# A third group's first layer by seven products, with sums made sooner and keys decayed on another engine

## Chip, cores, metric

One NeuronCore of a Trainium2 chip. The metric is device time in microseconds for one launch. Three runs of the kernel before gave 205.46, 205.52 and 206.92; their median is 205.52.

## What is computed

A linear attention with decay, then a two-layer network with the Mish activation. The attention has batch 4, 8 heads, 768 positions and 64 dimensions; the reference goes through the positions in blocks with a running state for each head:

```python
intra = np.einsum('bhic,bhjc->bhij', qb, kb) * Dmask[None]
intra = np.einsum('bhij,bhjd->bhid', intra, vb)
inter = np.einsum('bhid,bhde->bhie', qb * lam_pow[None], kv_state)
out[:, :, sl] = intra + inter
kb_dec = kb * rev_pow[None]
kv_state = lam_block[None, :, None, None] * kv_state + np.einsum('bhsd,bhse->bhde', kb_dec, vb)
...
x = attn_out.transpose(0, 2, 1, 3).reshape(B * S, H * D)     # 3072 x 512
h = x @ w_in                                                 # 512 -> 2048
g = h * np.tanh(sp)                                          # sp = log(1 + exp(h))
return (g @ w_out).astype(np.float32)                        # 2048 -> 512
```

## The kernel before

The order of the work is written out by hand: each engine runs its instructions in the order of the Python text, and waits only for data and for buffers.

**Groups.** The 768 positions are six groups of 128 (n = 0 to 5). A group has four batches, so 512 tokens. For each group there is attention (for each batch b), a first layer (512 -> 2048, sixteen slices of 128 outputs, Mish on ScalarE) and a second layer (2048 -> 512). "First group" is n = 0, "third group" n = 2.

**Attention of one batch.** `scores` (L250): 8 small matmuls into two PSUM banks, then VectorE multiplies each bank by the mask into `sb` (L260). `outputs` (L272): matmuls of the queries with the state, and of `sb` with the values, into one bank; VectorE scales them into `xn` (L284). `xn` is turned into the columns of `xt`, by a DMA on SP's queue (L287) or by TensorE in a function called later (L290 to L295). `state` (L299): matmuls of the decayed keys `kd` with the values (L302); VectorE adds the old state into `raw` (L310, two buffers); a multiplication by `lbm` writes the new state (L312). That last step is on GpSimd, but for batches 0 and 1 of the second group it is on VectorE and is called later (`decays1`). `decay_k` (L246) makes `kd` from the keys, with four buffers, on the engine that it is given. Keys and queries are turned by TensorE (`turn_pe`, L221) or, two batches at a time, by DMAs on SP's queue (`turn_dma`, L239). Keys, queries and values are fetched two batches at a time by DMAs on GpSimd's queue (`load_pair`, L84).

**First layer, two ways.** A plain `unit` (L337) is one slice of 128 outputs: 4 matmuls of 128 x 128 by 512 columns into one bank (L329), then Mish (L335). `two_units` (L348) does two slices for half the tokens. The other way (`set_of` to `set_step`, L392 to L448) takes four slices at a time as a 2 x 2 block product with seven products in place of eight, each of 4 matmuls by 256 columns (L412). A set needs sums of tokens (`x_sums`, L379, four VectorE operations for a group) and sums of weights (`w_sum`, L367, four for each quarter of w_in, made once). Its steps are m1; seed, a copy by ScalarE of the bank into a second bank (L426); m2; m5 with a copy by ScalarE (L434); m6 with a VectorE addition (L437); m7 with another (L441); m3; m4. Four sets make a group.

**Second layer.** The first group's is plain (L574). From the second on it has seven products, cut into fourteen halves of 8 matmuls (`dense2`, L529); one call of `h()` issues one half. It needs sums of w_out (`weight_sum`, L458, VectorE, eight in all) and of the tokens (`token_sum`, L471, called by `sums`).

**The loop** (L814, n = 1 to 4) weaves in each turn the second layer of group n, the first layer of group n + 1 and the attention of group n + 2. KINDS says for each turn and set whether the first layer is plain ("p") or by seven products ("s"): turn 1, which is the third group's first layer, is "pppp", the others "ssss". In an "s" turn the calls `opening`, `mm`, `closing` and `settle` set the steps of the sets among the halves; `held` keeps a `state` back to the next `s_`. Turn 1 also makes the sums of w_in for quarters 1 and 3 (WSUMS) and the last two `weight_sum`. Ahead of the loop, L715 to L801 write out the attention of the second and third groups, the second group's first layer by `two_units`, and the first group's second layer.

Of the kernel before, what the change touches and what calls it, by code (L numbers as in the profile page):

```python
# [7 lines left out]
F32 = mybir.dt.float32  # L8
# [12 lines left out]
def kernel(  # L21
# [276 lines left out]

    def state(n, b, tag, eng, later=False):  # L299
        pv = bank(tag, [JP, 128])  # L300
# [5 lines left out]
        if n == 0:  # L306
            nc.vector.tensor_tensor(out=w_new, in0=pv, in1=lbm, op=ALU.mult)
        else:
            raw = work.tile([128, JP, 128], F32, name="raw", tag="raw", bufs=2)
            nc.vector.tensor_tensor(out=raw, in0=pv, in1=wst[n, b], op=ALU.add)  # L310
            wst[n + 1, b] = w_new
            decay = lambda: eng.tensor_tensor(out=w_new, in0=raw, in1=lbm, op=ALU.mult)  # L312
            return decay if later else decay()
# [371 lines left out]
    def out1(b, turn, po, pv):  # L685
        later[b] = outputs(1, b, turn, po)
        return state(1, b, pv, nc.vector if b < 2 else nc.gpsimd, b < 2)

# [26 lines left out]
    turn1(2, "ze")  # L715
    turn1(3, "oB")
    two_units(1, 0, 0)
    scores(1, 2)
    for decay in decays1:
        decay()  # L720
    decay_k(1, 2, nc.vector)
    two_units(1, 2, 0)
    two_units(1, 4, 0)
    scores(1, 3)
    out1(2, "G", "z", "H")
    decay_k(1, 3, nc.vector)
    two_units(1, 6, 0)
    later[2]()
    out1(3, "G", "e", "o")
    two_units(1, 8, 0)  # L730
    later[3]()
    two_units(1, 10, 0)
    turn_pe(2, 0, ("H", "z"))
    decay_k(2, 0, nc.vector)
    decay_k(2, 1, nc.vector)
    w_sum(0, 0, nc.vector)
    w_sum(0, 1, nc.vector)
    two_units(1, 12, 0)
# [11 lines left out]
    two_units(1, 0, 1)  # L750
    w_sum(0, 2, nc.vector)
    w_sum(0, 3, nc.vector)
    turn_pe(2, 1, ("H", "G"))
# [19 lines left out]
    w_sum(2, 3, nc.vector)  # L773

# [23 lines left out]
    plain2(3, 0, 1, 2, 3)  # L798
    sums(1, 0, 2, 3)
    busy(1)  # L800
    halves = dense2(1)  # L801
# [8 lines left out]

    KINDS = {1: "pppp", 2: "ssss", 3: "ssss", 4: "ssss"}
    WSUMS = {(1, 0): (1,), (1, 1): (3,)}

    for n in range(1, NG - 1):  # L814
# [37 lines left out]
        def ws(n, i):  # L852
            for x in WSUMS.get((n, i), ()):
                for t in range(4):
                    w_sum(x, t, nc.vector)

# [67 lines left out]


        if "s" in kinds:
            x_sums(n + 1, 0, 1, 2, 3)
        opening(0)
        if m < NG:
            turn_dma(m, 1)  # L930
        if kinds[0] == "s":
            h(1)
            mm(0, "m2", "m5", "m6")
            sums(n, 1, 0, 1)
            h(1)
            o_(0)
            fetch(("k", 0), ("q", 0))
            closing(0)
        else:
            u(0)  # L940
            sums(n, 1, 0, 1)
            if n == 1:
                weight_sum(3, 0)
                weight_sum(3, 1)
            h(1)
            u(1)
            h(1)
            u(2)
            o_(0)
            fetch(("k", 0), ("q", 0))  # L950
            u(3)


        opening(1)
        h(1)
        if kinds[1] == "s":
            settle()
            mm(1, "m2")
            h(1)
            mm(1, "m5", "m6")  # L960
            sums(n, 1, 2)
            h(1)
            o_(1)
            fetch(("v", 0), ("k", 1))
            closing(1)
        else:
            u(8)
            settle()
            s_(1)
            sums(n, 1, 2, 3)  # L970
            ws(n, 0)
            h(1)
            u(9, 10)
            o_(1)
            fetch(("v", 0), ("k", 1))
            h(1)
            u(11)

# [7 lines left out]
        if kinds[2] == "s":  # L986
# [7 lines left out]
            h(1)  # L994
        else:
            u(4)
            settle()
            s_(2)
            u(5)
            ws(n, 1)  # L1000
            h(1)
            u(6)
            o_(2)
            fetch(("q", 1), ("v", 1))
            h(1)
            sums(n + 1, 0, 0, 1)
            h(1)
            u(7)


        opening(3)
        if kinds[3] == "s":
# [9 lines left out]
            sums(n + 1, 0, 2, 3)  # L1022
        else:
            s_(3)
            h(1)
            u(12)
            settle()
            h(1)
            o_(3)
            u(13)  # L1030
            sums(n + 1, 0, 2, 3)
            h(1)
            u(14)
        more = n + 1 < NG - 1
# [3 lines left out]
        if kinds[3] == "s":  # L1038
            if more:
                h(1)  # L1040
            settle()
        else:
            settle()
            u(15)
            if more:
                h(1)

# [32 lines left out]
```

## Time and profile before

| | |
|---|---|
| median of three runs | 205.52 us |
| the profiled execution | 206.36 us, of which 204.6 is the span of the profile |
| TensorE (PE) busy in the span | 193.8 us |
| VectorE (DVE) busy | 147.5 us |
| ScalarE (ACT) busy | 98.5 us |
| GpSimd (POOL) busy | 81.7 us |
| granted TensorE clock | 0.999 |

The profile's busy time of PE counts matmuls from issue to a modelled end, so neighbouring matmuls overlap; what one costs in a stream is the distance from its start to the next one's. PEld is the loading of weights, which overlaps PE. A row of a timeline gives start, length, engine, line, operation, output and inputs, how often, and in brackets how long the engine was idle before it and what ended that. "x2" is two operations one after the other in one row. GpSimd's DMA rows are the time that it takes to issue a transfer, not the transfer.

### The profile page before, as it was taken

What the parts mean: (1) busy time and instruction counts of PE and PEld (TensorE: products, weight loads), DVE (VectorE), ACT (ScalarE), POOL (GpSimd) and SP (SyncE); (2) the same over time, 40 slices, a digit from 0 to 9 for tenths busy, and PEclk for the clock granted to TensorE, in tenths of its full rate; (3) what the DMA queues carried; (4) which work ended last, traced back from release to release, by engine and by line L of the source; (5) the groups of instructions that cost most, each with busy time, mean ns of one, the idle gap of its engine ahead of it and who ended that gap; (6) DMA issues with size and microseconds to landing.
All of it is one profiled execution on the core that took longest, in us unless ns stands there. A gap on an engine that the chain in (4) does not pass through costs nothing.

```text
span 204.6 us, 4668 instructions
## 1 busy us (share of the span) xinstructions
PE 193.8 (95%) x1931; PEld 149.1 (73%) x1931; DVE 147.5 (72%) x247; ACT 98.5 (48%) x176; POOL 81.7 (40%) x78
## 2 busy tenths in 40 slices
PE   7869998979999999999999999999999999999990
PEld 3657455768865556667668888988988988888890
DVE  6696557698896977589868698799588657179041
ACT  4775663728631125343245662465474484826300
POOL 7998452472272591648684368230000000000020
PEclk9999999999999999999999999999999999999999
DMA  8999999999999999699999999994113211003123
GB/s 129 137 142 204 175 177 156 162 207 194 142 141 131 223 167 176 159 108 115 161 212 194 137 77 130 172 211 112 29 26 80 77 54 53 0 3 113 47 100 104
DMA packets 109336, 26.26 MB, mean 128 GB/s; under 512 B 99458, under 2 KB 108802, under 8 KB 109314
## 3 DMA queue, kind: packets, MB, share of 16 engines
q0 software_dynamic: 77568, 13.37, 88.5%
q1 hardware_dynamic: 30704, 12.33, 29.0%
q10 hardware_dynamic: 1042, 0.26, 0.6%
q8 instruction: 15, 0.25, 0.5%
q14 instruction: 7, 0.06, 0.1%
HBM read 27.26 MB, written 6.29 MB: 164 GB/s over the span
## 4 chain that ended last, share of the span: by engine, by line
PE 76%; DMA 9%; POOL 7%; DVE 3%; ACT 2%; issue 1%; POOLq 0%; DVEq 0%; ACTq 0%
PE bG L523 15%; PE bH L523 13%; DMA vn<-in_v_dram 8%; PE bB L412 6%; PE bC L412 5%; PE bA L412 4%; PE bA L329 3%; PE bB L329 3%; PE be L255 2%; PE bC L355 2%; POOL win L96 2%; PE bC L329 2%; PE bz L281 2%; PE bA L574 2%; PE bA L355 2%; PE bB L355 2%
## 5 line engine op out<-in xcount | busy, mean ns | idle before, releaser
L312 POOL TENSOR_TENSOR w<-raw,lbm 128x512 f16<-128x512 f32 x14 | 20.4, 1458 | 43.0 <-DVE raw L310 42.8
L523 PEld LDWEIGHTS <-gsum 128*128 128x128 f16 x336 | 31.2, 98 | 4.3
L523 PEld LDWEIGHTS <-hsg 128*128 128x128 f16 x240 | 23.0, 98 | 4.4
L605 POOL TENSOR_TENSOR c<-p,u 128x512 f32<-128x512 f32 x1 | 1.3, 1272 | 58.7 <-DVE p L604 58.7
L260 DVE TENSOR_TENSOR sb<-be,dm 128x512 f16<-128x512 f32 x22 | 15.1, 686 | 8.8 <-PE bo L255 8.1
L523 PE MATMUL bH<-tsum,gsum 128*128 128x256 f16 x160 | 20.4, 273 | 0.0
L329 PEld LDWEIGHTS <-win 128*128 128x128 f16 x136 | 12.6, 98 | 10.3 <-DMA win<-in_moe_w_in_dram 0.5
L412 PEld LDWEIGHTS <-wsum 128*128 128x128 f16 x192 | 18.5, 98 | 2.1
L523 PE MATMUL bG<-wout,hsg 128*128 128x256 f16 x160 | 19.9, 273 | 0.0
L412 PEld LDWEIGHTS <-win 128*128 128x128 f16 x144 | 13.8, 98 | 2.2 <-issue 0.5
L486 DVE TENSOR_TENSOR gsum<-hsg 128x1024 f16<-128x1024 f16 x20 | 15.1, 759 | 0.0
L284 DVE TENSOR_TENSOR xn<-bz,lq 128x512 f16<-128x512 f32 x18 | 12.3, 686 | 3.7 <-PE bz L281 3.7
L260 DVE TENSOR_TENSOR sb<-bo,dm 128x512 f16<-128x512 f32 x22 | 15.0, 680 | 0.0
L355 PEld LDWEIGHTS <-win 128*128 128x128 f16 x128 | 12.0, 98 | 1.6
L87 POOL DMA_DIRECT2D kn<-in_k_dram x10 | 11.8, 1182 | 2.8 <-PE bB L329 1.5
L87 POOL DMA_DIRECT2D qn<-in_q_dram x10 | 11.7, 1170 | 1.7 <-PE bA L329 0.9
L87 POOL DMA_DIRECT2D vn<-in_v_dram x10 | 11.6, 1164 | 1.4 <-DMA win<-in_moe_w_in_dram 1.4
L412 PE MATMUL bA<-xt,win 128*128 128x256 f16 x80 | 12.0, 272 | 0.1
L416 ACT ACTIVATE hsg<-bC 128x512 f16<-128x512 f32 x10 | 5.9, 593 | 11.7 <-PE bC L412 11.7
L329 PE MATMUL bA<-xt,win 128*128 128x512 f16 x44 | 11.3, 380 | 0.0
L574 PEld LDWEIGHTS <-hsg 128*128 128x128 f16 x64 | 6.1, 98 | 6.8
L335 ACT ACTIVATE hsg<-bA 128x512 f16<-128x512 f32 x11 | 6.6, 597 | 9.2 <-PE bA L329 9.2
(189 smaller groups left out, 442.3 us busy)
## 6 DMA issues: line engine op xcount, KB each, us to landing
out_dram<-osum SPq DMA_DIRECT2D x23, 256.0 KB, 2.8
kn<-in_k_dram POOLq DMA_DIRECT2D x10, 256.0 KB, 9.0
qn<-in_q_dram POOLq DMA_DIRECT2D x10, 256.0 KB, 7.1
vn<-in_v_dram POOLq DMA_DIRECT2D x10, 256.0 KB, 8.6
wout<-in_moe_w_out_dram POOLq DMA_DIRECT2D x4, 512.0 KB, 15.4
win<-in_moe_w_in_dram POOLq DMA_DIRECT2D x3, 512.0 KB, 10.8
vz<-in_v_dram POOLq DMA_DIRECT2D x2, 256.0 KB, 6.8
kn<-in_k_dram POOLq DMA_DIRECT2D x3, 128.0 KB, 4.7
```

What stands on the lines that cost most here:

```text
L87: nc.gpsimd.dma_start(out=tile_, in_=rows(src, n, 2 * bp, 2))
L260: nc.vector.tensor_tensor(out=sb[n, b, t], in0=p_[t], in1=dm[:, t], op=ALU.mult)
L284: nc.vector.tensor_tensor(out=xn, in0=po, in1=bc(lq, 2, D), op=ALU.mult)
L312: decay = lambda: eng.tensor_tensor(out=w_new, in0=raw, in1=lbm, op=ALU.mult)
L329: nc.tensor.matmul(open_[n, ni][:, lo:hi], win[ni // 4][:, kc, (ni % 4) * 128 : (ni % 4) * 128 + 128], xt[n][:, kc, lo:hi], start=(opens a ...
L335: nc.scalar.activation(h_tile(n)[:, ni, :], open_.pop((n, ni)), AF.Mish)
L355: nc.tensor.matmul(t[:, u, :], win[ni // 4][:, kc, m : m + 128], xt[n][:, kc, cs], start=(u == 0 and kc == 0), stop=(kc == NKC - 1), skip_ ...
L412: nc.tensor.matmul(t[:, u, :], lhs, rhs, start=(fresh and u == 0 and kk == 0), stop=(kk == 1), skip_group_check=True)
L416: nc.scalar.activation(h_tile(o.n)[:, 4 * o.s + 2 * r : 4 * o.s + 2 * r + 2, t * HC : t * HC + HC], src, AF.Mish)
L486: nc.vector.tensor_tensor(out=gsum[n, i][:, ks, :], in0=a, in1=b, op=op)
L523: nc.tensor.matmul(t, lhs(kk, blk), rhs(kk)[:, lo:hi], start=(fresh and kk == 0), stop=(kk == HK - 1), skip_group_check=True)
L574: nc.tensor.matmul(po, hsg[n][:, ki, b * C : (b + 1) * C], wout[part][:, kk, :], start=(ki == 0), stop=(ki == NKI - 1))
```

## The change

Turn 1 of the loop, the third group's first layer, uses seven products as well. All sums of w_in are therefore made ahead of the loop, in an order of quarters 0, 2, 1, 3 in which the sets need them. The third group's keys are decayed by GpSimd instead of VectorE, at other places in its queue. The second group's state decays for batches 0 and 1 stay on VectorE, but behind the masks of all four batches, and kd(1,2) goes ahead of scores(1,2). The sums `raw` of batches 2 and 3 of the second group use the buffers `p5` and `c22`. The first turn has an order of its own (`fresh`): it makes token sums of the second layer first, opens the first set, then makes the four token sums `x_sums`, and sets a half between m2 and m5. The branches of plain units are removed from the loop; they did nothing in the other turns.

```diff
-    def state(n, b, tag, eng, later=False):
+    def state(n, b, tag, eng, later=False, home=("raw", 2)):
...
-            raw = work.tile([128, JP, 128], F32, name="raw", tag="raw", bufs=2)
+            raw = work.tile([128, JP, 128], F32, name="raw", tag=home[0], bufs=home[1])
...
-        return state(1, b, pv, nc.vector if b < 2 else nc.gpsimd, b < 2)
+        return state(1, b, pv, nc.vector if b < 2 else nc.gpsimd, b < 2,
+                     ("raw", 2) if b < 2 else (("p5", "c22")[b - 2], 1))
...
     turn1(3, "oB")
+    decay_k(1, 2, nc.vector)
     two_units(1, 0, 0)
     scores(1, 2)
-    for decay in decays1:
-        decay()
-    decay_k(1, 2, nc.vector)
     two_units(1, 2, 0)
     two_units(1, 4, 0)
     scores(1, 3)
+    decay_k(2, 0, nc.gpsimd)
     out1(2, "G", "z", "H")
     decay_k(1, 3, nc.vector)
     two_units(1, 6, 0)
     later[2]()
     out1(3, "G", "e", "o")
+    for decay in decays1:
+        decay()
     two_units(1, 8, 0)
     later[3]()
     two_units(1, 10, 0)
     turn_pe(2, 0, ("H", "z"))
-    decay_k(2, 0, nc.vector)
-    decay_k(2, 1, nc.vector)
-    w_sum(0, 0, nc.vector)
-    w_sum(0, 1, nc.vector)
+    decay_k(2, 1, nc.gpsimd)
+    for i in range(4):
+        w_sum(0, i, nc.vector)
...
     two_units(1, 0, 1)
-    w_sum(0, 2, nc.vector)
-    w_sum(0, 3, nc.vector)
+    w_sum(1, 0, nc.vector)
+    w_sum(1, 1, nc.vector)
...
     attended(2, 1)
+    decay_k(2, 2, nc.gpsimd)
     for t, bp in (("k", 0), ("q", 0), ("v", 0)):
         load_pair(t, 3, bp)
+    decay_k(2, 3, nc.gpsimd)
...
-    w_sum(2, 0, nc.vector)
-    w_sum(2, 1, nc.vector)
-    w_sum(2, 2, nc.vector)
-    w_sum(2, 3, nc.vector)
+    for i in range(4):
+        w_sum(2, i, nc.vector)
+    w_sum(1, 2, nc.vector)
+    w_sum(1, 3, nc.vector)
...
     attend(2, 2)
-    decay_k(2, 2, nc.vector)
+    w_sum(3, 0, nc.vector)
+    w_sum(3, 1, nc.vector)
     plain2(1, 0, 1)
     attended(2, 2)
     turn_dma(3, 0)
     attend(2, 3)
-    decay_k(2, 3, nc.vector)
+    w_sum(3, 2, nc.vector)
+    w_sum(3, 3, nc.vector)
...
     sums(1, 0, 2, 3)
+    weight_sum(3, 0)
     busy(1)
     halves = dense2(1)
...
-    KINDS = {1: "pppp", 2: "ssss", 3: "ssss", 4: "ssss"}
-    WSUMS = {(1, 0): (1,), (1, 1): (3,)}
+    KINDS = {0: "pppp", 1: "ssss", 2: "ssss", 3: "ssss", 4: "ssss"}
...
+        fresh = kinds[0] == "s" and KINDS[n - 1][3] == "p"
+        if fresh:
+            sums(n, 1, 0, 1)
+            opening(0)
         if "s" in kinds:
             x_sums(n + 1, 0, 1, 2, 3)
-        opening(0)
+        if not fresh:
+            opening(0)
         if m < NG:
             turn_dma(m, 1)
         if kinds[0] == "s":
             h(1)
-            mm(0, "m2", "m5", "m6")
-            sums(n, 1, 0, 1)
-            h(1)
+            if fresh:
+                mm(0, "m2")
+                h(1)
+                mm(0, "m5", "m6")
+            else:
+                mm(0, "m2", "m5", "m6")
+                sums(n, 1, 0, 1)
+                h(1)
             o_(0)
             fetch(("k", 0), ("q", 0))
+            if fresh:
+                h(1)
             closing(0)
...
         opening(1)
-        h(1)
+        if not fresh:
+            h(1)
         if kinds[1] == "s":
             settle()
+            if n == 1:
+                weight_sum(3, 1)
             mm(1, "m2")
```

More of the change, by code (lines that the diff above doesn't have):

```diff
@@ L850, in fetch @@
                     load_pair(t, m + 1, bp)
[L852 to L855, printed above, removed]
         kinds = KINDS[n]
@@ L932 @@
             h(1)
-            mm(0, "m2", "m5", "m6")
-            sums(n, 1, 0, 1)
-            h(1)
+            if fresh:
[6 more added lines that the diff above has]
+                h(1)
             o_(0)
             fetch(("k", 0), ("q", 0))
+            if fresh:
+                h(1)
             closing(0)
[L939 to L944, printed above, removed]
-            h(1)
-            u(1)
-            h(1)
[L948 to L955, printed above, removed]
+        opening(1)
+        if not fresh:
+            h(1)
         if kinds[1] == "s":
             settle()
+            if n == 1:
+                weight_sum(3, 1)
             mm(1, "m2")
@@ L965 @@
             closing(1)
[L966 to L977, printed above, removed]
         opening(2)
@@ L994 @@
             h(1)
[L995 to L1008, printed above, removed]
         opening(3)
@@ L1022 @@
             sums(n + 1, 0, 2, 3)
[L1023 to L1033, printed above, removed]
         more = n + 1 < NG - 1
@@ L1041 @@
             settle()
[L1042 to L1046, printed above, removed]
     sums(NG - 1, 1, 2, 0, 1, 3)
```

## The prediction, made before the changed kernel ran

> **What bounds the kernel now.** I read the page's busy table and chain, then the windows by stage, then the timelines of TensorE, VectorE and GpSimd between 38 and 80 us.
>
> ```profile
> PE 193.8 (95%) x1931; PEld 149.1 (73%) x1931; DVE 147.5 (72%) x247; ACT 98.5 (48%) x176; POOL 81.7 (40%) x78
> PE 76%; DMA 9%; POOL 7%; DVE 3%; ACT 2%; issue 1%; POOLq 0%; DVEq 0%; ACTq 0%
> ```
> ```profile
> 32.80:58.80 26.00, 24.69 (x309) 20.48 (x306) 22.25 (x36) 15.04 (x27) 11.65 (x10) 1.00 1.87 171
> 58.80:75.07 16.27, 16.27 (x116) 8.16 (x114) 14.20 (x21) 2.52 (x5) 10.01 (x9) 1.00 1.43 171
> 75.07:107.20 32.13, 32.13 (x289) 21.98 (x288) 24.21 (x39) 12.39 (x21) 19.92 (x17) 1.00 1.69 153
> 107.20:135.90 28.70, 28.70 (x320) 25.03 (x318) 23.28 (x39) 14.54 (x26) 14.20 (x13) 1.00 1.47 149
> ```
>
> The columns of the windows are length, then busy time of PE, PEld, DVE, ACT, POOL, granted clock, DMA. TensorE sets the end: it is busy in all of 58.8 to 135.9 at a granted clock of 1.00, so a matmul saved there is time saved, if nothing makes it wait instead. The loop's turn that the change rewrites is 75.07 to 107.20; the next turn, 107.20 to 135.90, already does with the fourth group what the change does with the third. The other place is 32.8 to 58.8, where TensorE is 1.31 us short of full. Its three waits are all for VectorE:
>
> ```profile
> 41.58 0.40 PE L302 MATMUL bH<-vn,kd 128*128 128x128 f16 x4 [0.44 <-DVE kd L248]
> 43.38 0.40 PE L293 MATMUL bG<-ident,xn 128*128 128x128 f16 x4 [0.53 <-DVE xn L284]
> 44.58 0.40 PE L302 MATMUL bo<-vn,kd 128*128 128x128 f16 x4 [0.34 <-DVE kd L248]
> ```
>
> **The matmuls.** Four matmuls of 512 columns make a unit (L329); four of 256 make one step of the seven products (L412).
>
> ```profile
> 78.99 0.86 PE bB L329 x4
> 109.08 0.44 PE bA L412 x4
> ```
>
> 16 units at 0.866 (from the start-to-start of these rows' neighbours) are 13.86 us; 4 sets of 7 steps at 0.436 are 12.21. The change removes **1.65 us** of TensorE work. Four steps cost two 512-column matmuls' time each, so nothing is lost to the narrower shape. The Trainium skill, "TensorE: Matmul & The Clock Gate", section "Back-to-back issue gap", gives 131 ns as the sustained spacing of 512-column matmuls; by that the 64 old matmuls would be 8.4 us and the change a loss. The rows have 215 ns, so the rule does not hold here and enters below only as a rival.
>
> One wait comes with it. In the same place of a later turn, the second step of the first set waits for the copy that seeds the other bank: 136.99 plus 0.87 of work is 137.87, and m2 starts at 138.09.
>
> ```profile
> 136.99 1.05 PE L523 MATMUL bG<-wout,hsg 128*128 128x256 f16 x8
> 138.09 0.60 PE L412 MATMUL bA<-xt,win 128*128 128x256 f16 x4
> ```
>
> The old turn ended with a unit, so the turn after it had no old set to close and no such wait; now it has: **+0.2**.
>
> **The evictions.** Each set adds two VectorE additions, two ScalarE copies; the group adds four token sums.
>
> ```profile
> L437 DVE TENSOR_TENSOR bC<-bB,p 128x512 f32<-128x512 f32 x6 | 4.2, 700 | 5.9 <-PE bB L412 5.4 <-ACT p L434 0.5
> L390 DVE TENSOR_TENSOR xsum<-xt,xsum 128x512 f16<-128x512 f16 x6 | 2.5, 421 | 0.1
> L375 DVE TENSOR_TENSOR wsum<-win 128x512 f16<-128x512 f16 x8 | 4.2, 522 | 0.0
> ```
>
> VectorE gets 8 x 0.69 + 4 x 0.42 = 7.2 us, and loses eight sums of w_in (some 4.2 at the last row's mean) and a tsum and two gsum, which move ahead (1.9). That makes 24.21 + 7.2 - 6.1 = 25.3 of some 30.5 us, the share of the following turn (23.28 of 28.70), in which TensorE does not wait. ScalarE gets two copies a set and comes to about the following turn's share, 14.54 of 28.70. Hidden, at 0, once the turn is under way.
>
> **What moves ahead of the turn.** Here the two engines collide. A VectorE operation on SBUF alone stands still while GpSimd computes; one that reads PSUM does not.
>
> ```profile
> 57.20 2.36 DVE L467 TENSOR_TENSOR tsum<-wout,tsum 128x1024 f16<-128x1024 f16 x2
> 57.37 1.65 POOL L312 TENSOR_TENSOR w<-raw,lbm 128x512 f16<-128x512 f32 x1 [2.46 <-DVE raw L310]
> 44.44 0.68 DVE L284 TENSOR_TENSOR xn<-be,lq 128x512 f16<-128x512 f32 x1
> 44.01 1.64 POOL L312 TENSOR_TENSOR w<-raw,lbm 128x512 f16<-128x512 f32 x1 [1.21 <-DVE raw L310]
> ```
>
> Two tsum should take 1.2 (0.60 from start to start); they take 2.36, and GpSimd 1.65 instead of 1.27: each waits for the other's whole operation, in turn. So keys moved to GpSimd (1.03 us alone) are not simply gone from VectorE: each can hold up one of its SBUF operations by up to 1.03, against the 0.60 to 0.68 that VectorE saves.
>
> ```profile
> L248 POOL TENSOR_TENSOR kd<-kn,lk x8: 1032/1130/1601, 75.1 to 123.8; 128x512 f16<-128x512 f16 x8
> 41.65 1.15 POOL L87 DMA_DIRECT2D vn<-in_v_dram  x1
> ```
>
> The second group, 38 to 46. Before, VectorE ran the two state decays and kd(1,2) ahead of the masks of scores(1,3):
>
> ```profile
> 38.44 0.69 DVE L260 TENSOR_TENSOR sb<-be,dm 128x512 f16<-128x512 f32 x1 [0.90 <-PE bo L255]
> 39.64 1.28 DVE L312 TENSOR_TENSOR w<-raw,lbm 128x512 f16<-128x512 f32 x2
> 40.84 0.68 DVE L248 TENSOR_TENSOR kd<-kn,lk 128x512 f16<-128x512 f16 x1
> 43.84 0.68 DVE L248 TENSOR_TENSOR kd<-kn,lk 128x512 f16<-128x512 f16 x1
> 45.64 2.36 DVE L248 TENSOR_TENSOR kd<-kn,lk 128x512 f16<-128x512 f16 x2
> 40.37 0.22 PE L255 MATMUL bo<-qT,kT 64*128 64x128 f16 x1
> ```
>
> After, kd(1,2) fits into VectorE's 0.90 of idle time before 38.44, and the 0.44 wait goes. The last score matmul ends at 40.59, so the masks start at 40.62; at 0.60 from start to start xn follows at 41.82, raw at 42.42, and kd(1,3) would at 43.02, ending 43.70: the state matmuls at 43.76 instead of 44.58, **-0.82**. But GpSimd now has kd(2,0) in its queue where it used to wait for raw. It is free at 42.80, 0.2 us ahead of kd(1,3), so kd(1,3) stands until 43.83 and ends at 44.51. The matmuls then start at 44.57: **0.0**. Ends of this term: -1.31 (all waits go) and +0.5 (kd(1,3) behind two GpSimd operations). I take 0.0, since 42.80 comes ahead of 43.02 in these rows. Behind kd(2,0) in GpSimd's queue stands the decay of state (1,2), some 0.4 us later for it; the state is read next at 64, so nobody waits. That the sums raw of (1,2) and (1,3) lie in two other buffers costs nothing: the first set takes these after 79.
>
> From 45 to 62: VectorE loses two keys (2.36 with the wait) and gets two decays and two sums. The decays read SBUF twice in f32. No row shows such an operation beside GpSimd, so its hold-up is between 0 and one GpSimd operation (1.27). With it, VectorE reaches the masks of scores(2,0) at 50.55, about 1 us later, and has them at 51.83, where TensorE comes for them. Nothing to 0.1. The Trainium skill's "SBUF — State Buffer", section "Who interferes with whom", counts any VectorE operation with two SBUF inputs, f32 too; by it the 1.27 applies, and the sum stays the same. Later six sums replace four ahead of scores(2,2); kd(2,2) on GpSimd, after the decay at 57.37, costs one hold-up: VectorE arrives at 62.9 where it used to wait 1.59 us until 62.62.
>
> ```profile
> 51.83 0.40 PE L281 MATMUL bz<-vn,sb 128*128 128x64 f16 x8
> 62.62 0.69 DVE L260 TENSOR_TENSOR sb<-be,dm 128x512 f16<-128x512 f32 x1 [1.59 <-PE bo L255]
> 63.83 0.68 DVE L248 TENSOR_TENSOR kd<-kn,lk 128x512 f16<-128x512 f16 x1
> 68.19 0.40 PE L281 MATMUL bz<-vn,sb 128*128 128x64 f16 x8
> ```
>
> From 62 to 69: Sums of w_in stand where kd(2,2) and kd(2,3) stood, 0.75 for 0.60, and kd(2,3) on GpSimd falls on the first pair, +1.0. The masks of scores(2,3) end at 68.35 where TensorE wants them at 68.19: **+0.2**. On GpSimd's queue the three loads of the fourth group go 1.6 us later (one key and its wait for the port). Issued at 60.6, landing 9 us on, transposed 4.5 to 4.9 us on, the last is there by about 76 for scores(3,0) at 77.1; on SP's queue the transposes only follow. Hidden with some 1 us to spare; without it, what is short is paid.
>
> ```profile
> kn<-in_k_dram POOLq DMA_DIRECT2D x10, 256.0 KB, 9.0
> kT<-kn SPq DMA_TRANSPOSE x7, 4.5
> ```
>
> From 69 to 80: VectorE runs 1.1 us late from here, through this:
>
> ```profile
> 70.54 1.64 DVE L486 TENSOR_TENSOR gsum<-gsum,hsg 128x1024 f16<-128x1024 f16 x1
> 72.11 1.52 DVE L467 TENSOR_TENSOR tsum<-wout,wout 128x1024 f16<-128x1024 f16 x1
> 73.56 1.52 DVE L486 TENSOR_TENSOR gsum<-hsg 128x1024 f16<-128x1024 f16 x1
> 75.00 0.68 DVE L486 TENSOR_TENSOR gsum<-hsg,gsum 128x1024 f16<-128x1024 f16 x1
> 75.08 2.50 POOL L248 TENSOR_TENSOR kd<-kn,lk 128x512 f16<-128x512 f16 x2
> 77.18 0.69 DVE L260 TENSOR_TENSOR sb<-be,dm 128x512 f16<-128x512 f32 x1 [1.49 <-PE bo L255]
> ```
>
> The slack ahead of the masks was 1.49. The change puts one tsum and two gsum there (1.8), and the two GpSimd keys then fall among them. The two rows of 1.52 are explained by no GpSimd computation (it was issuing loads, which slow no other row of their kind). If they become 0.60 at their new offsets, the masks run at 78.0 and the first token sums are there at 79.7 and 80.05; TensorE comes to m5 at 79.85 and to m6 at 80.3: **0.0**. If both stay, the keys come ahead of three sums, the masks run at 80.75, and m5 waits until 82.45: +2.6. I take 0.0: the same forms take 0.68 in nearly all other rows; both ends stay in the range.
>
> **Sum**: -1.65 + 0.2 + 0.0 + 0.2 + 0.0 = -1.25, against the profiled run's 206.36 (span 204.6 and 1.76 around it), 205.1. The three runs shown have a median of 205.52; with it, **204.3 us**.
>
> **The rivals.**
> A, the forecast: 204.3, between 203.8 and 204.9.
> B, the front wait goes too: kd(1,3) gets ahead of kd(2,0) because GpSimd's loads end after 43.02. For it: the margin is 0.2 us, and the loads' pace hangs on earlier landings. Against: the rows as they stand. It gives -0.82 more and takes the 0.2 of 68.19 away: 203.3.
> C, slower: a new wait at the first set's m5, for token sums behind masks, weight sums and GpSimd's two keys. It decides as soon as VectorE finishes the masks of scores(3,0) later than about 79.3. For it: the two rows of 1.52, and 1.49 of slack against 1.8 of added work. Its price is up to 2.6: half of it 205.6, all of it 206.9.
> D, the change does not pay: the narrow steps run no faster than the units, as by the 131 ns, or the turn is as long as before for some other reason: 205.5 or more. The next turn's 28.70 against 32.13 speaks against it.
>
> **Chances.** A 0.38, B 0.27, C 0.33 (0.19 half, 0.14 full or beyond), D 0.02. One per cent, 2.05 us, is about what a measurement of this kernel can tell from no change. B's lower half and the case that all 1.31 goes lie beyond it: faster 0.27. C with a second wait, such as late keys for scores(3,0), lies above 207.6: slower 0.07. Else within: 0.66. The range runs from B's 203.3 with half of the remaining front wait gone, 202.8, to C's full price, 206.9. The likeliest case alone has 203.8 to 204.9.
>
> **What would show it.** In the changed profile: L329 only for the first group, 28 more steps of L412 at 0.44; the turn from the first masks to the next m1 about 1.4 us shorter; kd(1,3) on VectorE 1.4 us or more long, beside a GpSimd kd at 42.8, and state(1,3) near 44.6 (A) or 43.8 (B); a wait of TensorE at the first L412 that reads xsum of 0 to 0.2 (A) or 1 to 2.6 (C); the lengths of the tsum and gsum between 72 and 76. Wrong in its reasons, whatever the time, if kd(1,3) is not held up, or if TensorE waits for the m6 additions.

## The result, and the profile after

The changed kernel takes 209.68 us (median of six runs, 207.38 to 210.70) beside 205.79 for the kernel before in the same comparison: a ratio of 1.014, with an interval of 1.009 to 1.019. The ratio leaves out the slowest run, 210.70, and is not the quotient of the two medians. It is slower. The forecast was 204.3, with a range of 202.8 to 206.9. The profiled execution took 209.72 us with a span of 207.9 (before: 206.36 and 204.6).

The busy table and the windows by stage of the changed kernel, at the places that answer to those shown of before (the front; the first group's second layer; turn 1 of the loop; turn 2):

```profile
PE 195.4 (94%) x1979; PEld 156.0 (75%) x1979; DVE 159.4 (77%) x255; ACT 102.0 (49%) x184; POOL 86.9 (42%) x82
```
```profile
31.45:60.20 28.75, 25.98 (x309) 21.40 (x306) 25.65 (x38) 15.04 (x27) 13.76 (x12) 0.94 1.84 172
60.20:76.55 16.35, 16.35 (x115) 8.19 (x114) 16.25 (x24) 2.53 (x5) 11.82 (x11) 1.00 1.23 132
76.55:109.36 32.81, 30.89 (x337) 26.67 (x336) 28.50 (x43) 15.33 (x28) 18.32 (x15) 1.00 1.71 161
109.36:139.75 30.39, 29.36 (x321) 25.07 (x319) 25.69 (x40) 15.32 (x28) 17.11 (x15) 1.00 1.49 144
```

The second number is the length, the third TensorE's busy time. Before, the two turns were full (32.13 of 32.13, 28.70 of 28.70). Now turn 1 has 1.92 us without a matmul and turn 2 has 1.03, and the front misses 2.77, at a granted clock of 0.94. Which loss belongs where is easier to see between fixed matmuls, since the head of the run hangs on when the first transfers land. The trace gives the starts of the first matmul of `two_units`, of the first half (L523) of turns 1 and 3, and the end:

| from, to | before | after | difference |
|---|---|---|---|
| head, to the first `two_units` | 37.04 | 35.70 | -1.34 |
| front, to the first half of turn 1 | 37.86 | 40.68 | +2.82 |
| turn 1, to the first m1 of turn 2 | 32.25 | 32.93 | +0.68 |
| turn 2 from there, to the first half of turn 3 | 26.79 | 28.47 | +1.68 |
| the rest | 70.63 | 70.17 | -0.46 |

**The front.** The timelines of VectorE, GpSimd and TensorE around kd(1,3), changed kernel:

```profile
41.68 2.73 DVE L248 TENSOR_TENSOR kd<-kn,lk 128x512 f16<-128x512 f16 x1
41.59 1.05 POOL L248 TENSOR_TENSOR kd<-kn,lk 128x512 f16<-128x512 f16 x1
42.59 1.27 POOL L312 TENSOR_TENSOR w<-raw,lbm 128x512 f16<-128x512 f32 x1
44.47 0.61 PE L302 MATMUL bo<-vn,kd 128*128 128x128 f16 x4 [2.40 <-DVE kd L248]
44.88 1.92 PE L355 MATMUL bA<-xt,win 128*128 128x256 f16 x8
```

VectorE's kd(1,3) comes 0.09 us behind GpSimd's kd(2,0), and stands through that and through the state decay queued behind it: 2.73 us in place of 0.68. TensorE waits 2.40. Then the eight matmuls of 256 columns take 1.92 us, where they take 1.04 elsewhere. The windows by microsecond say why; the column after the five busy times is the granted clock:

```profile
44.00:45.00 1.00, 0.53 (x5) 0.53 (x6) 1.00 (x2) 0.00 (x0) 0.00 (x0) 0.59 1.23 204
45.00:46.00 1.00, 1.00 (x7) 0.69 (x6) 0.90 (x3) 0.00 (x0) 0.11 (x1) 0.50 1.24 206
46.00:47.00 1.00, 1.00 (x8) 0.82 (x7) 1.00 (x2) 0.17 (x1) 1.00 (x1) 0.50 1.24 206
47.00:48.00 1.00, 1.00 (x10) 0.81 (x8) 1.00 (x1) 0.91 (x2) 1.00 (x2) 0.71 1.23 204
```

From state(1,3) to the fourth `two_units` behind it, 3.52 us before are 5.02 now: 1.50 us for the clock. It seems not to fall in each run. The two runs with a mean granted clock of 0.996 and 1.000 took 207.38 and 207.64, the four with 0.992 took 209.64 to 210.70. That the fall makes all of the 2.2 us between them is not shown: one run was traced, and its trace accounts for 1.50.

**Turn 1, first set.** VectorE, GpSimd and TensorE ahead of m5:

```profile
74.28 1.52 DVE L467 TENSOR_TENSOR tsum<-wout,wout 128x1024 f16<-128x1024 f16 x1
75.73 1.52 DVE L486 TENSOR_TENSOR gsum<-hsg 128x1024 f16<-128x1024 f16 x1
77.78 1.53 DVE L467 TENSOR_TENSOR tsum<-wout,tsum 128x1024 f16<-128x1024 f16 x1
79.23 1.52 DVE L486 TENSOR_TENSOR gsum<-hsg 128x1024 f16<-128x1024 f16 x1
73.76 1.21 POOL L87 DMA_DIRECT2D kn<-in_k_dram  x1
77.26 2.95 POOL L248 TENSOR_TENSOR kd<-kn,lk 128x512 f16<-128x512 f16 x2
83.06 0.60 PE L412 MATMUL bC<-xsum,wsum 128*128 128x256 f16 x4 [1.72 <-DVE xsum L390]
```

The two rows of 1.52 are there as before, two more come beside GpSimd's keys, and the token sums `xsum` are late: m5 waits 1.72 us.

**Turn 2, its start.** The same three engines, changed kernel:

```profile
108.16 1.65 POOL L312 TENSOR_TENSOR w<-raw,lbm 128x512 f16<-128x512 f32 x1 [3.56 <-DVE raw L310]
109.77 2.68 POOL L248 TENSOR_TENSOR kd<-kn,lk 128x512 f16<-128x512 f16 x2
110.28 1.26 DVE L390 TENSOR_TENSOR xsum<-xt 128x512 f16<-128x512 f16 x1
111.58 1.15 DVE L390 TENSOR_TENSOR xsum<-xt,xsum 128x512 f16<-128x512 f16 x1
112.78 0.60 PE L412 MATMUL bB<-xsum,wsum 128*128 128x256 f16 x4 [0.47 <-DVE xsum L390]
```

And the kernel before:

```profile
104.91 2.48 POOL L248 TENSOR_TENSOR kd<-kn,lk 128x512 f16<-128x512 f16 x2
107.91 0.42 DVE L390 TENSOR_TENSOR xsum<-xt 128x512 f16<-128x512 f16 x1 [2.42 <-DMA xt<-xn]
```

Before, GpSimd was done with kd(4,0) and kd(4,1) at 107.39, ahead of the token sums. In an "s" turn `held` keeps the last state(3,3) back until the last set is closed, so its decay and the two keys behind it on GpSimd's queue come later, and fall on the sums: 1.26 and 1.15 us in place of 0.42. TensorE then waits 0.47, 0.15, 0.23 and 0.12 us, one after the other.

### The profile page after: what moved, and what is told of

It reads as the page before. It is cut to its first block, busy times and chain, and to the rows that moved or that the text cites. A ratio compares the mean times of both kernels' runs of the same rounds, so it can differ in the third digit from the quotient of the medians.

```text
span 207.9 us, 4797 instructions
## 1 busy us (share of the span) xinstructions
PE 195.4 (94%) x1979; PEld 156.0 (75%) x1979; DVE 159.4 (77%) x255; ACT 102.0 (49%) x184; POOL 86.9 (42%) x82
## 4 chain that ended last, share of the span: by engine, by line
PE 70%; DVE 9%; DMA 7%; POOL 7%; ACT 3%; issue 2%; POOLq 0%; DVEq 0%; ACTq 0%
PE bH L523 13%; PE bG L523 12%; PE bB L412 7%; DMA win<-in_moe_w_in_dram 6%; PE bC L412 6%; PE bA L412 5%; PE bA L355 3%; PE be L255 2%; PE bB L355 2%; PE bC L355 2%; DVE gsum L486 2%; POOL win L96 2%; PE bA L574 2%; PE bz L281 2%; PE bz L276 2%
## 5 line engine op out<-in xcount | busy, mean ns | idle before, releaser
L523 PEld LDWEIGHTS <-gsum 128*128 128x128 f16 x336 | 31.3, 98 | 3.5
L412 PEld LDWEIGHTS <-wsum 128*128 128x128 f16 x256 | 24.7, 98 | 5.7 <-issue 2.9
L523 PEld LDWEIGHTS <-hsg 128*128 128x128 f16 x240 | 22.8, 98 | 3.2
L412 PEld LDWEIGHTS <-win 128*128 128x128 f16 x192 | 18.4, 98 | 3.3 <-issue 1.0
L523 PE MATMUL bH<-tsum,gsum 128*128 128x256 f16 x160 | 20.4, 273 | 0.0
L523 PE MATMUL bG<-wout,hsg 128*128 128x256 f16 x160 | 19.8, 273 | 0.0
L412 PE MATMUL bA<-xt,win 128*128 128x256 f16 x112 | 16.8, 272 | 0.2
L416 ACT ACTIVATE hsg<-bC 128x512 f16<-128x512 f32 x14 | 8.3, 594 | 16.4 <-PE bC L412 16.3
L486 DVE TENSOR_TENSOR gsum<-hsg 128x1024 f16<-128x1024 f16 x20 | 16.0, 802 | 0.0
L248 POOL TENSOR_TENSOR kd<-kn,lk 128x512 f16<-128x512 f16 x12 | 14.9, 1244 | 0.0
L355 PEld LDWEIGHTS <-win 128*128 128x128 f16 x128 | 12.7, 103 | 2.1 <-issue 0.2
L412 PE MATMUL bB<-xsum,wsum 128*128 128x256 f16 x88 | 13.2, 272 | 0.7 <-DVE xsum L390 0.5
L412 PE MATMUL bC<-xsum,wsum 128*128 128x256 f16 x80 | 12.0, 272 | 1.7 <-DVE xsum L390 1.7
L416 ACT ACTIVATE hsg<-bB 128x512 f16<-128x512 f32 x14 | 8.3, 596 | 8.0 <-PE bB L412 5.7
```

Source lines behind the costliest of these rows:

```text
L248: eng.tensor_tensor(out=kd[n, b], in0=kn[n, b], in1=bc(lk, 2, D), op=ALU.mult)
L355: nc.tensor.matmul(t[:, u, :], win[ni // 4][:, kc, m : m + 128], xt[n][:, kc, cs], start=(u == 0 and kc == 0), stop=(kc == NKC - 1), skip_ ...
L412: nc.tensor.matmul(t[:, u, :], lhs, rhs, start=(fresh and u == 0 and kk == 0), stop=(kk == 1), skip_group_check=True)
L416: nc.scalar.activation(h_tile(o.n)[:, 4 * o.s + 2 * r : 4 * o.s + 2 * r + 2, t * HC : t * HC + HC], src, AF.Mish)
L486: nc.vector.tensor_tensor(out=gsum[n, i][:, ks, :], in0=a, in1=b, op=op)
L523: nc.tensor.matmul(t, lhs(kk, blk), rhs(kk)[:, lo:hi], start=(fresh and kk == 0), stop=(kk == HK - 1), skip_group_check=True)
```

## The experiments

Theory: there are three separate losses. kd(1,3) behind two GpSimd operations (T1, with the fall of the clock behind it); the first set's token sums behind sums that GpSimd slows (T2); the keys of turn 2 on its token sums (T3). Rival: the third group's keys on GpSimd are the whole loss, wherever it shows. A second rival is that the seven products themselves don't pay.

The stretches in us, front, turns 1 and 2 together, and the rest, from the trace of each run, with the time and the ratio to the kernel before on the same chip:

| | front | turns 1, 2 | rest | sum | median us | ratio, interval |
|---|---|---|---|---|---|---|
| before | 37.86 | 59.04 | 70.63 | 167.53 | 205.5 to 205.8 | |
| after | 40.68 | 61.40 | 70.17 | 172.25 | 209.68 | 1.014 (1.009 to 1.019) |
| e1 | 37.77 | 61.40 | 70.19 | 169.36 | 207.30 | 1.007 (1.005 to 1.010) |
| e2 | 40.54 | 60.38 | 70.19 | 171.11 | 208.28 | 1.010 (1.004 to 1.016) |
| e3 | 37.05 | 59.04 | 70.59 | 166.68 | 204.78 | 0.996 (0.994 to 0.999) |
| e4 | 37.91 | 61.62 | 70.17 | 169.70 | 207.76 | 1.010 (1.008 to 1.013) |
| f1 | 37.78 | 62.39 | 70.18 | 170.35 | 208.60 | 1.014 (1.008 to 1.020) |
| f2 | 37.50 | 61.41 | 70.20 | 169.11 | 207.20 | 1.008 (1.004 to 1.011) |
| f3 | 37.77 | 59.92 | 70.19 | 167.88 | 205.68 | 0.999 (0.997 to 1.002) |
| f4 | 37.18 | 59.52 | 70.19 | 166.89 | 205.56 | 0.998 (0.995 to 1.002) |
| g1 | 37.17 | 58.91 | 70.17 | 166.25 | 204.59 | 0.995 (0.992 to 0.998) |
| g2 | 38.12 | 58.90 | 70.20 | 167.22 | 204.97 | 0.998 (0.995 to 1.001) |
| g3 | 37.77 | 65.84 | 70.21 | 173.82 | 211.66 | one run |

The runs of a version differ in mean clock (after: 0.992 to 1.000), so versions are compared by the stretches of their traces.

**e1, the change with GpSimd's kd(2,0) moved behind the two state decays.**

```diff
-    decay_k(2, 0, nc.gpsimd)
     out1(2, "G", "z", "H")
...
+    decay_k(2, 0, nc.gpsimd)
     decay_k(2, 1, nc.gpsimd)
```

> The changed kernel with one move: kd(2,0) stands behind the state decays of (1,2) and (1,3) in GpSimd's queue, beside kd(2,1). Theory 1 (VectorE's kd(1,3) is locked out by two GpSimd operations in a row, and TensorE's clock falls in the idle time that follows): kd(1,3) takes about 0.7 instead of 2.73 us, the 2.4 us wait of the state matmuls falls to under 0.5, the granted clock stays at 1.00 between 44 and 48, and the time falls by 2.0 to 3.9 us from the changed kernel's 209.7, to 205.8 to 207.7. Rival (the seven-product turn with its evictions is what is slow, the wait at 44 is made good later): it stays above 209.

VectorE and TensorE in e1:

```profile
42.31 0.68 DVE L248 TENSOR_TENSOR kd<-kn,lk 128x512 f16<-128x512 f16 x1
43.05 0.40 PE L302 MATMUL bo<-vn,kd 128*128 128x128 f16 x4 [0.34 <-DVE kd L248]
```

kd(1,3) takes 0.68, the wait of 2.40 is 0.34, and the clock stays at 1.00. From the first `two_units` to state(1,3) it is 6.72 us, 0.82 less than before. The front's +2.82 is gone, and only that: turns 1 and 2 stand at 61.40 to the hundredth. T1 holds. But the front as a whole, 37.77, is no shorter than before's 37.86: most of the 0.82 is lost again behind state(1,3), where TensorE now waits twice for masks, 0.27 and 0.11 us, and did not before:

```profile
50.76 0.38 PE L281 MATMUL bz<-vn,sb 128*128 128x64 f16 x7 [0.27 <-DVE sb L260]
```

**e2, the change with `x_sums` ahead of the other token sums of turn 1, and `weight_sum(3, 0)` behind.**

```diff
-    weight_sum(3, 0)
     busy(1)
...
-            sums(n, 1, 0, 1)
             opening(0)
         if "s" in kinds:
             x_sums(n + 1, 0, 1, 2, 3)
+        if fresh:
+            sums(n, 1, 0, 1)
...
+                weight_sum(3, 0)
                 weight_sum(3, 1)
```

> The changed kernel with the token sums of the first layer ahead of the second layer's two sums and of the last sums of w_out in the first turn's VectorE order (weight_sum(3,0) goes beside weight_sum(3,1)). Theory 1 (the wait of 1.9 us at the first step that reads token sums is VectorE's queue, drawn out by two key operations of GpSimd): that wait falls under 0.5 and the time by 1.2 to 1.9, to about 208; the wait at 44 stays. Rival (the wait is for the outputs of attention, landed late by DMA, or for the addition m6): the wait stays and so does the time, 209.7.

The wait at m5 is gone, but not all of its 1.72 comes back: turns 1 and 2 gain 1.02. The row that takes it back, with the clock of e2's front, where the wait of T1 is still 2.09 us:

```profile
90.68 0.60 PE L412 MATMUL bC<-xsum,wsum 128*128 128x256 f16 x4 [0.58 <-DVE bB L437]
```
```profile
46.00:47.00 1.00, 1.00 (x9) 0.85 (x7) 1.00 (x2) 0.31 (x1) 1.00 (x1) 0.50 1.25 208
```

VectorE pays for the sums later, in the second set, where an eviction is then late. T2's place is right; the cure is worth 1.0.

**e3, the kernel before with the new order of the front alone** (kd(1,2) first, the state decays behind all masks, the two other buffers for `raw`; keys stay on VectorE).

```diff
...
+    decay_k(1, 2, nc.vector)
     two_units(1, 0, 0)
     scores(1, 2)
-    for decay in decays1:
-        decay()
-    decay_k(1, 2, nc.vector)
...
     out1(3, "G", "e", "o")
+    for decay in decays1:
+        decay()
```

> The kernel before with one part of the change: kd(1,2) ahead of scores(1,2), the two state decays behind all masks, the two other buffers for raw; keys of the third group stay on VectorE, the third group's first layer stays plain. Theory 1 (the order of VectorE is better, and only GpSimd's kd(2,0) spoils it): the waits of 1.31 us between 41 and 45 fall to about 0.5, and the time to 204.8 to 205.2. Rival (the order itself delays kd(1,3)): a wait over 1 us at the state matmuls of (1,3), and a time of 206 or more.

From the first `two_units` to state(1,3) it is again 6.72 us, and the front is 0.81 shorter; the whole is 0.4% faster. The part of the change that concerns VectorE alone does what it should.

**e4, the change with before's front, and all keys of the third group on VectorE where they were.**

```diff
...
-    decay_k(2, 1, nc.gpsimd)
+    decay_k(2, 0, nc.vector)
+    decay_k(2, 1, nc.vector)
...
     attend(2, 2)
+    decay_k(2, 2, nc.vector)
...
```

> The changed kernel with the front of before: the third group's keys on VectorE at their old places, the state decays and kd(1,2) at their old places. What is left of the change is the seven-product turn with the sums made sooner. Theory 1: 1.65 us of matmuls saved, a wait of 1 to 2 us at the first token sums (GpSimd's two keys of the fourth group fall among VectorE's sums there), and about 0.9 us of waits at the opening of the following turn (keys of the fifth group among the token sums): 205.5 to 207. Rival (all of the loss comes from the third group's keys on GpSimd): 204.2.

```profile
80.28 0.60 PE L412 MATMUL bC<-xsum,wsum 128*128 128x256 f16 x4 [1.94 <-DVE xsum L390]
```

Without any key of the third group on GpSimd, m5 waits 1.94 and turns 1 and 2 are as long as after. The time, 207.76, lies above the 205.5 to 207 expected. The rival falls: these keys cost the front, not the turns.

**f1, e1 with the loads of the fourth group's second pair issued right behind those of the first**, so that no load stands beside the sums at 72 to 76.

```diff
     decay_k(2, 3, nc.gpsimd)
+    for t, bp in (("k", 1), ("q", 1), ("v", 1)):
+        load_pair(t, 3, bp)
...
     attended(2, 3)
-    for t, bp in (("k", 1), ("q", 1), ("v", 1)):
-        load_pair(t, 3, bp)
```

> E1 (kd(2,0) later) with one more move: the three loads of the fourth group's second pair of batches go right behind those of the first pair, so GpSimd issues no load between its last state decay of the third group and the two keys of the fourth. Theory 1 (the two VectorE operations of 1.52 us are held up while GpSimd issues loads at that place): both become about 0.68, VectorE gains up to 1.7 us, and the wait at the first step that reads token sums falls from 1.7 to under 0.5; about 1.2 to 1.7 us under E1's 207.3. Rival (the 1.52 belong to those instructions or to other transfers): they stay, and so do the wait and the time.

This was missed. f1 is slower than e1. The scores of turn 1 now wait for their queries, TensorE's row and the landing of that transpose in the DMA issues of 58 to 76, f1:

```profile
78.57 0.21 PE L255 MATMUL be<-qT,kT 64*128 64x128 f16 x1 [2.82 <-DMA qT<-qn]
```
```profile
qT<-qn SPq DMA_TRANSPOSE x1, 10.9
```

In e1 the same transpose lands in:

```profile
qT<-qn SPq DMA_TRANSPOSE x1, 4.0
```

The first pair's loads land no later (the queries 7.3 us after their issue in both runs), and this transpose is issued at nearly the same time (67.64 in f1, 68.12 in e1). But in f1 the second pair's loads are in flight beside it, and it takes 6.9 us more. The wait at m5 is replaced by a longer one ahead of it. The two rows of 1.52 stayed too, since GpSimd's keys moved up beside them:

```profile
72.40 1.53 DVE L467 TENSOR_TENSOR tsum<-wout,wout 128x1024 f16<-128x1024 f16 x1
73.85 1.52 DVE L486 TENSOR_TENSOR gsum<-hsg 128x1024 f16<-128x1024 f16 x1
71.89 2.94 POOL L248 TENSOR_TENSOR kd<-kn,lk 128x512 f16<-128x512 f16 x2
```

**f2, the change with kd(1,3) ahead of kd(2,0)** and of what `out1(2)` gives VectorE.

```diff
+    decay_k(1, 3, nc.vector)
     decay_k(2, 0, nc.gpsimd)
     out1(2, "G", "z", "H")
-    decay_k(1, 3, nc.vector)
```

> The changed kernel with kd(1,3) on VectorE ahead of the scaling xn(1,2) and the sum raw(1,2) instead of behind them; GpSimd has the same work in the same order. Theory 1 (which of the two engines comes first to the port decides): kd(1,3) runs at about 40.5 for 0.68, the wait of 2.4 us at the state matmuls goes, one of some 0.9 us at the turning of xn(1,2) stays in its place, the clock stays at 1.00, and the time is 2 to 3.5 us under the changed kernel's 209.7. Rival (any key of the third group on GpSimd at this place costs the 2.4): the state matmuls still wait over 1.5.

The front is 37.50, so the order of two operations on two engines was worth 3.2 us of it. With e1 this settles T1 from both sides.

**f3, e1 with the keys of turn 2 a set sooner on GpSimd's queue.**

```diff
-                if b == 0 and not last:
+                if b == 0 and not last and n == 1:
...
-                if b < B - 1:
+                if b < B - 1 and (n == 1 or b > 0):
...
+        if n == 1:
+            decay_k(m + 1, 0, nc.gpsimd)
+            decay_k(m + 1, 1, nc.gpsimd)
         opening(3)
```

> E1 with one more move: the fifth group's first two keys are issued on GpSimd ahead of the last step of the loop's first turn, and no longer at the opening of the second turn. Theory 1 (the second turn's waits come from these two keys, which lock out the token sums there because the seven-product order holds the last state decay of the turn back): the token sums at the opening of the second turn take 0.42 each, the waits there go, and the time is 1.2 to 1.7 us under E1's 207.3. Rival (the second turn waits for attention landed late by DMA, since TensorE now arrives sooner): its waits stay.

GpSimd and VectorE in f3:

```profile
98.31 2.75 POOL L248 TENSOR_TENSOR kd<-kn,lk 128x512 f16<-128x512 f16 x2
108.26 0.41 DVE L390 TENSOR_TENSOR xsum<-xt 128x512 f16<-128x512 f16 x1
```

The sums take 0.41 again, none of the four waits of turn 2 is left, and turns 1 and 2 are 1.48 shorter. T3 holds.

**f4, e4 with e3's front, f1's early loads and f3's keys.**

> All that the runs so far speak for: E3's front (order of the change, keys of the third group on VectorE), the seven-product turn of the change with its sums made sooner, F1's early loads and F3's early keys. Theory 1 (three port collisions are the whole loss): -0.8 from the front, -1.65 from the matmuls, +0.2 to 0.5 of what stays, against the kernel before: 203.2 to 203.9 where that has 205.6. Rival (evictions and sums of the seven-product turn weigh on VectorE by themselves): no better than E3, 204.8 or more.

Missed: the early loads give it f1's wait (1.44 us for the queries), and it ties with before.

**g1 and g2, all three places mended without early loads.** g1 is e4 with e3's front, e2's order and f3's keys; g2 is f2 with e2's order and f3's keys, so its third group's keys are on GpSimd.

> The version with before's keys on VectorE, the masks ahead of the decays, x_sums ahead of the other token sums of the first turn, and the keys kd(4,0), kd(4,1) of the second turn issued a set sooner. From the first two_units to the last instruction, by the traces of the runs that had one mend each: 37.2 us of front (f4), 28.3 us of the first turn (e2), 29.2 us of the second turn (f3), 70.2 us of the rest, together 164.9 us against 167.5 us of before: ratio 0.987, some 203.0 us. Theory: the three waits are separate, so mending them adds up. Rival: they are not, since VectorE and GpSimd have as much work as before and what is mended in one place stands in the next; then the ratio is 0.995 or more, as it was for e3 and for f4.

> The change as it was made, with the third group's keys on GpSimd, and three mends: kd(1,3) ahead of kd(2,0), x_sums ahead of the other token sums of the first turn, kd(4,0) and kd(4,1) a set sooner. 37.5 us of front (f2), 28.3 us (e2), 29.2 us (f3), 70.2 us: 165.2 us against 167.5 us, ratio 0.989, some 203.3 us. If the keys on GpSimd cost more elsewhere than the trace of f2 shows, it is slower than g1 by more than 0.5 us.

g1's stretches are 37.17, 58.91 and 70.17, and those of the runs with one mend each make 37.18 (f4), 29.73 + 29.17 (turn 1 of e2, turn 2 of f3) and 70.19, which is 166.27 beside 166.25: the mends add up. (Turn 1 ends here at the first half of turn 2, so that the two parts join.) The expectations of g1 and g2 had put turn 1 of e2 at 28.3 by a slip of subtraction; with 29.73 the ratio for g1 would have been 0.993, and 0.995 was measured (0.992 to 0.998). g1 is the fastest version of the change, 0.5% faster than before. But e3, which has no seven products in turn 1, is 0.4% faster, and the two can't be told apart: in turns 1 and 2 g1 is 0.13 us shorter than e3. So the second rival is nearly right for the whole, though not for the matmuls. From start to start, some 1.5 us of first-layer matmuls are saved; 0.69 come back as two waits (0.11, 0.58), some 0.46 in the halves (the seeds among it), some 0.2 in the attention's matmuls. The longer wait, in the groups of g1:

```profile
L412 PE MATMUL bC<-xsum,wsum 128*128 128x256 f16 x80 | 12.0, 273 | 0.6 <-DVE bB L437 0.6
```

g2's front is 0.95 longer than g1's, and 0.62 longer than that of f2, which has the same order of work there. kd(1,3) comes ahead of xn in VectorE's order and takes 1.31 in g2, 0.68 in f2:

```profile
40.67 1.31 DVE L248 TENSOR_TENSOR kd<-kn,lk 128x512 f16<-128x512 f16 x1
40.26 1.14 POOL L87 DMA_DIRECT2D vn<-in_v_dram  x1 [0.25 <-PE bH L302]
41.42 1.46 POOL L248 TENSOR_TENSOR kd<-kn,lk 128x512 f16<-128x512 f16 x1
42.64 0.40 PE L293 MATMUL bG<-ident,xn 128*128 128x128 f16 x4 [1.55 <-DVE xn L284]
```

By these stamps kd(1,3) would have ended at 41.35, ahead of kd(2,0), and is held up beside the issue of a load with a decay of keys behind it. In f2 it starts at 40.51, just ahead of that issue at 40.58. So even with this order the front hangs on some tenths of a microsecond.

**g3, f1 with kd(3,0) and kd(3,1) on VectorE behind the first set's outputs**, so that GpSimd computes nothing beside the sums.

```diff
-                if b == 0 and not last:
+                if b == 0 and not last and n > 1:
...
-                if b < B - 1:
+                if n == 1 and b == 0:
+                    decay_k(m, 0, nc.vector)
+                    decay_k(m, 1, nc.vector)
+                elif b < B - 1:
```

> f1 with kd(3,0) and kd(3,1) made by VectorE behind o_(0) of the first turn, so that GpSimd has nothing from the end of the state decay near 72 us to the loads of the fourth turn's keys. If it is GpSimd's instructions beside them that make two sums of 1024 elements take 1.52 us (loads in e1, keys in f1), both take 0.68 us here, and VectorE is done with the sums near 75.5 us instead of 77.9 us. If they take 1.52 us again, GpSimd is not the cause of these two rows.

```profile
72.84 0.68 DVE L467 TENSOR_TENSOR tsum<-wout,wout 128x1024 f16<-128x1024 f16 x1
73.44 0.68 DVE L486 TENSOR_TENSOR gsum<-hsg 128x1024 f16<-128x1024 f16 x1
72.31 1.21 POOL L87 DMA_DIRECT2D kn<-in_k_dram  x1
79.51 0.26 PE L255 MATMUL be<-qT,kT 64*128 64x128 f16 x1 [3.32 <-DMA qT<-qn]
```

These sums take 0.68, beside issues of loads, and VectorE is done with them at 76.65. So GpSimd's computing made the rows of 1.52 in f1. What makes them in before, after and e1, where loads stand beside the first two, is not settled: in all of these two decays of keys stand behind the loads in GpSimd's queue, in g3 none does, but no run changed that alone. With one decay behind the load both occur: kd(1,3) of g2 above is held up, while a gsum of before at 86.44 takes its 0.68. As in f1, the queries come late (3.32 us), and the clock falls behind that wait, so g3's time says nothing about its order.

## Why the prediction was wrong

The forecast of 204.3 was 5.4 us too low, and the time lies beyond the end of the range, in a case that was given 0.07: rival C's wait with others besides it. One of the others is a term that the prediction had and mis-sized, the front; one it did not have, the start of turn 2.

**The matmuls, -1.65.** Right in kind, a little large. In turn 1 of before, the 64 plain matmuls take 14.12 us from start to start; in turn 2 of f3, which waits for nothing, 112 narrow ones take 12.61. That makes 1.51 saved. The narrow steps run nearly as fast as the units by column (0.440 and 0.431 ns), so rival D's reason fell.

**The seed, +0.2.** Right: the 112 matmuls of the halves in turn 2 take 12.46 after and 12.22 before.

**The evictions, 0.** Right in turn 1 of the changed kernel but for 0.20 us (an m7 addition, L441). The prediction named a wait for an m6 addition (L437) as a sign that its reasons are wrong, and there are such waits: 0.23 at the start of turn 2, where the token sums are late, and 0.58 in turn 1 once the token sums come first (e2, g1).

**The front, "I take 0.0".** This step failed. The gain of 0.82 was exact (e1, e3: 7.54 to 6.72), and that kd(1,3) meets kd(2,0) was foreseen, with a margin of 0.2 us that was 0.09. The hold-up was wrong. I let kd(1,3) go on after one GpSimd operation; it stood through both, 2.05 us over its 0.68, since the state decay of (1,2) had its data at 41.76 and was next in the queue at 42.59. The upper end of +0.5, named for just this, was too small: state(1,3) came +1.23. The prediction's own rows gave that much: two operations, of 1.03 and 1.27, from 42.80 end at 45.10, with the 0.68 of kd(1,3) and 0.06 to the matmuls that is 45.84 in place of 44.58, or +1.26. The rows that I drew "in turn" from (2.36 for two VectorE operations) show that the engines can alternate, not that they must. At 109.77 of the changed kernel two keys are ready on GpSimd and a token sum does get its turn between them; what decides it is not known. The fall of the clock, +1.50, was in no case of mine.

The Trainium skill, "SBUF — State Buffer", section "SBUF: two separate sides", says that of a GpSimd operation and a VectorE operation with two SBUF inputs, whichever starts first gets the shared port pair for the whole instruction and the other blocks fully. For kd(2,0), 0.09 us ahead, the rows agree. For the next operation, which got its turn ahead of a kd(1,3) that had stood for 0.9 us, it says nothing.

**45 to 62, nothing; 62 to 69, +0.2.** Right. From the first `two_units` for the second half of the tokens to the first matmul of the second layer it is 9.24 us in both kernels, and the next stretch, to the first half of turn 1, grew from 16.26 to 16.35. But there TensorE comes later, by the wait and the fall of the clock. In f2, which has neither and the same keys on GpSimd, the stretches are 9.32 and 16.55, so the terms are +0.08 and +0.29, near enough. In e1 they are 9.67 and 16.55: moving kd(2,0) back costs 0.35 in the first. In g1, with the third group's keys on VectorE, they are 9.32 and 16.31. So even without a collision at kd(1,3), keys on GpSimd take back 0.2 to 0.6 of the 0.82. The f32 decays, for which no row was at hand, are held up by GpSimd like the others:

```profile
45.73 2.36 DVE L312 TENSOR_TENSOR w<-raw,lbm 128x512 f16<-128x512 f32 x2
45.89 1.65 POOL L312 TENSOR_TENSOR w<-raw,lbm 128x512 f16<-128x512 f32 x1 [2.03 <-DVE raw L310]
```

**69 to 80, 0.0 with ends 0 and +2.6.** The wrong end was taken. The rows of 1.52 had stood there for a reason that I couldn't name, and I let them vanish. They stayed, the keys cost two more, and the wait of 1.72 lies inside rival C's price. A long row without a known cause should have been carried over as it stands.

**What was not in the sum.** Turn 2, +1.68. I costed what an "s" turn adds to VectorE and ScalarE, and not that `held` in it delays the last state, hence its decay, and the next turn's keys queued on GpSimd. The prediction used turn 2 of before as the model of a turn without waits; it was one because the turn ahead of it was plain. The rest of the run is 0.41 to 0.46 shorter in all versions with the loop's change. TensorE's part of it is 65.82 us in every run, so the difference lies behind its last matmul, where the last outputs are written; its cause stays open.

Together: -1.51 + 0.2 for the seven products, against +1.23 + 1.50 in the front, some 1.9 in turn 1 (the waits of 1.72 and 0.20), some 1.5 in turn 2 beside the 0.2, and -0.46 at the end. That is 4.4 of the 4.72 us; the rest is small ends.

## What to carry to other kernels

When work is moved to an engine that holds up the one that feeds the bottleneck, place it by what else is ready behind it in that queue: here one operation a tenth of a microsecond ahead let two go first. When a stage is replaced by another kind, look at what it releases at its end, and whether the next stage relied on that being early. Earlier loads aren't free: with the second pair's loads in flight, the first pair's transposes came late.

## What the hardware showed

**The granted clock falls to half behind a wait of 2.1 to 3.3 us, sometimes, and the traces show when.** It stood at 0.50 from 44.17 to 47.58 after a wait of 2.40 (changed kernel), from 44.70 to 48.11 after 2.09 (e2), and from 78.30 to 85.12 after 3.32 (g3). It did not fall after 2.82 in f1. The falls last 3.41 us, or twice that, and the times at full clock are multiples of it too: in f1 from 6.05 to 204.02, which is 58 x 3.413. So the clock changes on a grid of 3.41 us, which lies otherwise in each run. The stretch of the grid ahead of the fall in the changed kernel, e2 and g3, then two stretches of f1 (the second number is the length, the third TensorE's busy time, the eighth the clock, counts in brackets aside):

```profile
40.76:44.17 3.41, 1.00 (x18) 0.74 (x16) 3.41 (x3) 1.19 (x2) 3.08 (x3) 1.00 1.25 206
41.29:44.70 3.41, 1.06 (x20) 0.94 (x21) 3.41 (x4) 1.17 (x2) 2.57 (x3) 1.00 1.24 202
74.89:78.30 3.41, 1.30 (x12) 1.01 (x11) 1.73 (x3) 1.08 (x2) 0.00 (x0) 1.00 1.84 153
```
```profile
74.32:77.73 3.41, 1.43 (x14) 1.12 (x12) 3.38 (x5) 1.08 (x2) 2.81 (x3) 1.00 1.57 202
77.73:81.14 3.41, 2.57 (x29) 2.24 (x29) 2.30 (x6) 0.60 (x1) 0.00 (x0) 1.00 1.25 228
```

TensorE was idle for 2.41, 2.35 and 2.11 us of the stretch ahead of a fall. The edge at 77.73 cuts f1's wait in two, and neither stretch has more than 1.98. In all thirteen traces, from the first rise of the clock to the end, half clock follows each of the twelve full-clock stretches with 2.11 us or more of idle time, and none with 1.98 or less. So what counts in these traces is not the length of a wait but how much idle time falls into one stretch, with the limit between 1.98 and 2.11 us. By that, the same wait of 2.40 can cost a fall in one run and none in another. In g3 the stretch behind the fall has 1.21 us idle, and the next is at half clock as well. In the changed kernel and e2 it has 0.30 and nothing, and the clock is back. f1's four runs fit (207.50 and 207.74 at mean clocks of 1.000 and 0.995, 209.46 and 209.89 at 0.989 and 0.988), but one of them alone was traced.

The Trainium skill, "TensorE: Matmul & The Clock Gate", section "Part 1: The HAM clock gate", has a window of 3.4 us that runs freely, a half and a full state, and an idle window as what halves the clock. The half state, the grid and the difference between runs agree with that; that 2.1 us of idle time in a window are enough is more than it says. What was not tried is a wait of set length.
